# A fused attention and gated feed-forward kernel: the warm-up of TensorE as one chain of five groups, and a new written order

## The chip, the cores and the metric

The kernel runs on one core of one Trainium2 chip. A core has five engines, each with a queue of its own that it works through in order: PE (TensorE, matrix products, with PEld for its weight loads), DVE (VectorE), ACT (ScalarE), POOL (GpSimd) and SP (SyncE, which here only issues transfers). SP, ACT and POOL can issue DMA transfers; all of them run on the same 16 DMA engines. The metric is the device time of one execution, in microseconds, as the median of several runs.

## The reference

Two stages. The first is an attention in Nyström form for 8 batches of 8 heads, 576 tokens of 64 values: queries and keys are averaged over groups of 18 tokens into 32 landmarks, three softmax matrices are built, and the small one, 32 x 32, is inverted by six steps of an iteration.

```python
q_lm = q.reshape(B, H, m, S // m, D).mean(axis=3)
k_lm = k.reshape(B, H, m, S // m, D).mean(axis=3)
A = sm(q, k_lm); Bm = sm(q_lm, k_lm); C = sm(q_lm, k)
Z = Bm.T / (norm_1(Bm) * norm_inf(Bm) + 1e-06)
for _ in range(6):
    Z = 2 * Z - Z @ Bm @ Z
attn = A @ Z @ C @ v
```

The second takes the 4608 tokens of 512 values through a multiplicative feed-forward layer:

```python
a = x @ w1; b = x @ w2
out = (a * b @ w3) @ w_out
```

## The kernel before

**Parts.** `w3 @ w_out` is formed once on the chip: the products `mm{j}{c}` (j and c from 0 to 7) accumulate `w34`. Both factors are split into a high and a low half-precision part. For that, pieces of `w_out` (loads `wf0` to `wf3`, half issued by SP, names ending in `s`, half by ACT, ending in `a`, two DMAs each) go through `woh` and `wos` on ACT and `wol` on POOL; pieces of `w3` (loads `w3n0` to `w3n7`, on SP, half of the first on ACT) go through a transposition `tr` on DVE, `wh` and `ws` on ACT and `wl` on POOL. `mm{j}{c}` is three matmuls: high by high, high by low, low by high. So `mm00` needs `wh00`, `woh0` for its first matmul, `wol0` for its second and `wl00` for its third; `mm01`, `mm02`, `mm03` need `wol1`, `wol2`, `wol3`.

The attention works on 16 quads (four heads of one batch; n from 0 to 15). Loads `lq{n}0` and `lq{n}1` bring k and q, issued by POOL; `lv{n}` brings v, issued by SP. DVE transposes them (`T`), PE sums 18 rows for the landmarks of the first six quads (`mp{n}`, 18 matmuls; POOL does it for the others, `ma` and `mb`), ACT scales the sums (`mk`), DVE transposes those (`lt`), PE forms the scores (`S`, `A`), and the softmax passes through DVE (`sm`, `ar`, `am`, `au`), POOL (`as`, `an`) and ACT (`se`, `ae`). Then come the 32 x 32 iteration (`N`, `x`, `Z` on PE, `y` on DVE), the products with v (`C`), with w1 and w2 (`W`, `U`), the dense products (`d` on PE, `e` on ACT, `f` on DVE) and the output (`g` on PE, `h` on ACT, stores `st` on SP).

**Order.** Every step is a task with a name, an engine and a function. The string ORDER lists all of them; `Plan.run` reads names and buffer slots from it, and the kernel issues the tasks in just that order, so that each engine's queue is the part of ORDER that belongs to it. The dependencies, durations and due times that `add` is given are for the planner with which the order was made; `Plan.run` uses of a task its function and the names of its buffers (`acq`). What a task waits for on the chip follows from the tiles that it reads and writes. The number after a colon is a slot: a PSUM bank for PE's tasks, a buffer otherwise.

```python
def run(self):
    order = []
    for word in ORDER.split():
        name, _, slots = word.partition(":")
        t = self.by[name]
```

**Warm-up.** `zz` zeroes a tile on DVE, and `wu0` to `wu3` multiply it by itself, six matmuls of 128 x 512 each, into banks that nothing reads. `ca`, `cb`, `cc` build the identity and other constants on DVE, POOL and DVE. `gw0` to `gw3` are copies of one column on POOL; each reads the last bytes of a `wf` load, and so holds back what POOL issues behind it.

**The first tasks of each queue**, as ORDER before has them:

```
PE   wu2 wu3 wu0 wu1 mm00 mm01 mm02 mm03 mp0 mm04 mm05 mm06 A0 mm10 S0 mp1 mm07
ACT  w3n0a.0 w3n0a wf0a.0 wf0a wf1a.0 wf1a wf2a.0 wf2a wh00 ws00 woh1 wos1 wf3a.0 wf3a woh2 woh0
POOL cb gw0 wl00 wol1 gw1 lq00 lq01 lq10 lq11 wol0 wl01 wol2 wol3 wol4 gw2 wol5 gw3 wol6 wl10 lq20
DVE  tr00 ca zz tr01 cc tr10 T00 T01 tr11 lt0
SP   w3n0.0 w3n0 wf0s.0 wf0s wf1s.0 wf1s wf2s.0 wf2s w3n1 (4) wf3s.0 wf3s w3n2.0 w3n2.1 lv0.0
```

Of the kernel before, what the change touches and what calls it, by code (L numbers as in the profile page):

```python
# [44 lines left out]
woh7 A0:6.7 lq20:2 mm10:0 wos7 lq21 ar0:0 w3n3 ws11 S0:1.2 wol7 w3n4.0:1 T11 mp1:3 lv0.2 am0:0 lq30:3 w3n4.1
mm07 sm0:1 mk1:1 w3n4.2 as0 mm11 w3n4 tr20:0.0 sw0 mm12 wl11 lt1 ae0 tr21:1 mm13 wh20 au0 w3n5.0:2 lq31 wh21
A1:5.6 ws20 w3n5.1 S1:7.3 sb0 ar1:1 an0:0 ws21 mm14 se00:0 am1:2 mm15 wl20 se01 mm16 sm1:3 w3n5.2 mm17 as1 T20:0
sw1 ct0:0 mm20:5 wl21 ae1 mm21 tr30:2.1 wo0 aT0:0 mp2:6 w3n5 lq40:0 bo0:0 sb1 T21 lq41 mm22 au1 mk2:0 lq50:1
mm23 lq51 mm24 se10:1 lt2 lq60:2 T30:1 wh30 A2:1.2 lq61 tr31:3 ws30 mm25 lw00 T31 bo1 w3n6.0:0 mm26 wo1 wl30
w3n6.1 ar2:0 se11 mm27 lv0 wh31 an1:1 N0:4.4 w3n6.2 am2:5 wo2 S2:6.7 lv1.0:1 ws31 bt0 mm30:0 tr40:0.0 w3n6 as2  # L50
mm31 lv1.1 ct1:1 wh40 mp3:3 sm2:6 lw11 ae2 tr41:1 lw01 mp4:1 mk3:1 lv1.2 au2 wl31 mm32 ws40 T40:0 mm33 lq70:3
wh41 aT1:1 lq71 sw2 mk4:0 mm34 w3n7.0:1 sb2 lt3 an2:0 no0:0 mm35 se20:0 A3:2.5 ws41 wl40 lt4 T41 mm36 bo2:1 mm37
ar3:1 lv1 lw10 mm40:3 wl41 wo3 am3:7 S3:1.6 w3n7.1 tr50:2.1 x0_0:4 as3 A4:2.5 sm3:8 wh50 mm41 T50:1 ws50 lq80:0
sw3 mm42 ae3 tr51:3 ma6:0 w3n7.2 mp5:0 sb3 T51 ar4:0 mm43 w3n7 mk5:1 mm44 au3 wl50 se21 S4:2.5 am4:9 wh51 mm45
an3:1 lv2.0:2 se30:1 mm46 ct2:2 ws51 mm47 sm4:0 as4 bo3 lv2.1 se31 mm50:0 lt5 wo4 y0_0:1 tr60:0.0 sw4 lq81
A5:7.1 lv2.2 ct3:3 lq90:1 wh60 mm51 wl51 ae4 tr61:1 mm52 ws60 ar5:1 mm53 lq91 lv2 aT3:2 mm54 wl60 am5:2 mm55 au4
lv3.0:3 mm56 as5 S5:6.4 sb4 T60:0 x0_1:3 mb6 ae5 C0:1.7 sm5:4 wh61 lv3.1 au5 ws61 bo4 se40:0 T61 mm57 T70:1 wl61
sw5 mk6:0 mm60:2 lv3.2 co0:0.5 mm61 an4:1 lt6 mm62 y0_1:2 sb5 T71 se50:1 mm63 ma7:0 lv3 wo5 aT4:3 A6:1.7
tr70:2.1 bo5 se51 x0_2:3 N1:6.7 wh70 lv4.0:0 y0_2:0 ct5:0 S6:0.4 ws70 x0_3:3 an5:1 bt1 mm64 se41 ar6:0 lv4.1
mm65 no1:1 wl70 mm66 lv4.2 mm67 mb7 tr71:3 y0_3:2 x1_0:5 wh71 T80:0 lv4 x0_4:1 mm70:7 ws71 y1_0:0 y0_4:1 mm71  # L60
aT5:4 lv5.0:1 sm6:1 x1_1:6 wl71 mk7:1 Z0:3 am6:3 sw6 mm72 lv5.1 sb6 y1_1:2 as6 se60:1 mm73 lt7 zo0:0 se61 ct4:1
S7:5.1 lv5.2 ma8:0 ae6 W0:6 sm7:5 mm74 wp0:0 wo6 T81 lv5 A7:0.3 mm75 ar7:1 mb8 sw7 C1:4.2 T90:1 sb7 au6 se70:0
am7:9 bo6:0 se71 mm76 lv6.0:2 wq0 as7 T91 lv6.1 mk8:0 mm77 lv6.2 co1:1.2 U000:0.3.0.1 lv6 lq100:2 wo7 U011:5.1
lv7.0:3 aT2:5 ae7 U010:6.2 ma9:0 lt8 lv7.1 ct6:2 C2:4.7 uo0001 lv7.2 uo0110 ct7:3 lv7 uo0101 au7 uo0000 an6:1
uo0100 U001:3.5 uo0111 co2:0.7 lv8.0:0 S8:2.0 lv8.1 uo0011 lq101 d000:6.1 lv8.2 sm8:6 bo7 mb9 uo0010 lv8
d002:4.7 e000:0 lv9.0:1 sw8 f000:0 A8:5.3 lv9.1 e002:1 sb8 d021:6.1 f002:1 se80:1 lv9.2 ar8:0 d011:4.7 se81 lv9
e021:2 T100:0 d020:2.0 an7:0 am8:8 x1_2:3 e020:0 lq110:3 e011:1 d022:5.6 f021 mk9:1 lq111 f011 d001:2.4 y1_2:1
as8 f020 d010:1.7 e022:2 e001:1 f022 d032:3.5 e010:0 ma10:0 lt9 ae8 f001 d031:0.2 f010 e032:2 x1_3:6 e031:1 T101
d012:1.4 f032 lq120:0 d030:3.7 y1_3:0 e012:0 f031 lq121 A9:0.5 e030:2 aT7:0 lq130:1 x1_4:6 f012 mb10 S9:1.2
ar9:1 g30:3 sm9:2 g31 am9:0 g20:4 y1_4:2 T110:1 as9 sw9 mk10:0 f030 Z1:0 aT6:1 g21 sb9 ct8:0 ae9 ma11:0 g10:5  # L70
lt10 h3:0 zo1:1 h2:1 S10:6.7 au8 se90:0 W1:3 W2:0 au9 mb11 C3:4.1 wp2:1 wp1:0 bo8 se91 wq1 bo9 sm10:4 wq2 T111
U100:2.3.2.3 lv10.0:2 N2:0.3 lv10.1 ct9:1 uo1001 an8:0 lv10.2 uo1000 sw10 co3:1.7 g11 lv10 mk11:1 an9:1 lv11.0:3
bt2 A10:3.2 sb10 no2:1 lv11.1 se100:1 g00:1 lv11.2 ma12:0 h1:2 lv11 ar10:0 U110:4.6 se101 st1.0 U200:0.5.0.1
uo1101 lt11 st1 am10:9 x2_0:7 uo2001 st2.0 S11:2.3 uo2000 y2_0:0 as10 U210:6.5 T120:0 uo1100 A11:7.0 uo2100
sm11:1 g01 lq131 uo2101 T121 ae10 mb12 sw11 d200:4.6 sb11 ar11:1 se110:0 x2_1:5 h0:3 U201:2.0 se111 y2_1:2
U111:7.1 ct10:2 uo2010 x2_2:5 am11:5 e200:1 uo1110 d100:3.2 f200:2 as11 uo1111 U211:4.7 y2_2:1 e100:0 au10
U101:6.1 mk12:0 lq140:2 C4:5.3 f100 ae11 ma13:0 uo1011 au11 uo2111 uo1010 d101:2.1 lv12.0:0 lt12 uo2011 co4:0.8
st3.0 S12:7.6 lq141 e101:2 x2_3:0 lv12.1 uo2110 f101:3 lq150:3 d112:3.5 lv12.2 sm12:7 mb13 st3 d132:2.4 e112:1
y2_3:0 st0.0 sw12 f112 d121:1.3 e132:0 lv12 sb12 T130:1 se120:1 d111:0.5 lv13.0:1 e121:2 f132 st0 d202:2.7 se121
st2 e111:1 d110:1.4 e202:0 lv13.1 f111 d120:6.0 f121 e110:1 d130:2.5 f110 d231:3.1 T131 e130:2 e120:1 f202:0  # L80
x2_4:4 mk13:1 f120 d222:2.6 f130 d131:7.0 y2_4:2 e222:0 ma14:0 e231:1 d232:5.4 f222 e131:2 f231 d211:2.3 f131
d210:6.7 e211:0 e232:1 d122:1.0 f211 bo10:1 e210:2 d102:2.5 bo11 f210 e122:0 g60:3 aT8:2 e102:2 an10:0 f102
d201:6.1 ct11:3 g61 e201:2 mb14 f201 Z2:7 A12:2.5 zo2:0 d230:6.1 f122 T140:0 g50:7 e230:2 h6:2 ar12:0 lq151
d221:0.6 mk14:0 lt13 g40:3 am12:0 e221:0 lt14 g80:2 as12 T141 g70:5 f232 f221 g81 aT9:5 f230 d220:0.4 h8:0 g41
st8.0 ma15:0 st6.0 W4:6 h4:3 W3:1 st8 ae12 g71 lv13.2 wp3:1 e220:1 lv13 wq3 d212:2.3 ct12:0 st4.0 an11:1 g110:0
e212:0 f220 wp4:0 f212 h7:1 A14:1.2 mb15 g51 ar14:1 U300:4.3.2.3 aT10:3 h5:0 wq4 S14:5.1 uo3001 am14:3 st5.0
S13:2.7 uo3000 g90:6 st4 sm13:2 as14 st6 T150:0 g111 st7.0 sm14:6 ae14 sw13 st7 g91 sb13 T151 st5 se130:0 g120:3
au12 g121 au14 bo12 an12:0 h11:3 g100:4 h12:2 sw14 se131 g101 mk15:1 ct13:1 A13:2.0 sb14 aT11:4 h9:1 C6:3.7
ar13:0 se140:1 h10:0 am13:8 bo14:0 se141 lt15 as13 U301:6.0 co6:0.9 lv14.0:0 U400:2.5.0.1 lv14.1 uo3010 an14:1
U410:4.1 st11.0 uo4000 S15:3.7 ae13 lv14.2 C5:6.2 st12.0 uo4100 au13 uo4001 lv14 uo4101 lv15.0:1 sm15:5 uo3011  # L90
st10.0 bo13 U411:4.5 co5:1.0 st9.0 N3:1.2 uo4111 lv15.1 uo4110 sw15 st12 bt3 A15:0.2 sb15 no3:1 se150:0 lv15.2
d412:6.5 st10 se151 d402:4.3 ar15:1 e412:2 st11 x3_0:1 e402:1 st9 U401:7.6 f402:3 d400:0.2 uo4011 f412 uo4010
am15:7 d410:4.3 e400:0 d411:5.6 as15 e410:1 f400:1 d430:7.0 y3_0:0 e411:2 f410 d420:4.2 ae15 d422:1.5 e430:0
e420:1 f430 d431:3.7 f420 d432:4.0 f411 au15 g180:2 e432:0 e422:1 d421:6.4 e431:2 f422 g181 f431 e421:1 f432
f421 x3_1:1 h18:2 U311:3.5 st18.0 U310:7.6 g210:0 uo3100 uo3101 g211 uo3111 d310:4.2 h21:0 d401:7.6 st21.0
e310:2 uo3110 d300:5.0 f310 bo15 y3_1:2 e401:0 d321:4.3 f401 d301:2.1 e321:1 N4:7.9 e301:2 x3_2:6 e300:0 f301:2
d322:4.2 bt4 y3_2:1 d330:5.1 no4:0 e322:2 g190:6 f322 d320:4.7 f300 aT14:2 g191 e320:2 an15:1 f320 d311:2.0 f321
g200:4 e311:0 f311 d302:7.3 ct15:0 g201 e302:2 ct14:1 h19:3 d331:2.0 h20:1 d312:7.6 e330:1 st20.0 e331:0 f330
d332:4.5 st19.0 e312:1 g130:2 st18 f312 st21 aT12:5 g140:1 e332:1 f302 st19 an13:0 f331 g141 st20 x3_3:7 x4_0:6
# [940 lines left out]
```

## Time and profile before

| | us |
|---|---|
| median of 3 runs | 273.0 |
| lowest and highest | 271.47, 273.58 |
| profiled execution | 273.78 |
| its span | 272.0 |
| PE, DVE, ACT, POOL busy | 256.0, 179.7, 173.6, 137.6 |

The rows of the page and of the views that matter stand in the prediction. Times in them are from the start of the span. A timeline row is: start, length, engine and line, operation, written and read tile, how many instructions were merged, and in brackets how long the engine had been idle and what ended that. An engine's name with a q (ACTq, SPq) is its sequencer, which issues DMAs. Almost all matmuls have one line, L244, so tiles tell them apart: `bank<-aT` is the warm-up, `bank<-wo,w3t` the `mm` products, `bank<-nat,ident` the `mp` sums. `w3n`, `u` and `ab` are also the tiles into which weights are first loaded; `nat` takes k and q.

### The profile page before, as it was taken

To read this page: it belongs to the slowest core of one execution; us is meant where nothing else is said; L and a number is where in the kernel's file an instruction comes from. 1 tells how busy PE (TensorE), PEld (TensorE's weight loads), DVE (VectorE), ACT (ScalarE), POOL (GpSimd) and SP (SyncE) were. 2 spreads that over 40 slices of the span, in tenths; PEclk is the share of its full clock that TensorE was granted. 3 is DMA by queue.
4 is the path that set the end of the run, shared out by engine and by line. 5 is a ranking of instruction groups with operands and counts; after the bars stand their busy time and mean duration, and the time that the engine had idled before them with its cause. 6 is when DMAs were issued, how large, how long until landed. Compare 5 with 4: busy or idle time off the path is not lost.

```text
span 272.0 us, 9712 instructions
## 1 busy us (share of the span) xinstructions
PE 256.0 (94%) x4020; PEld 171.0 (63%) x4020; DVE 179.7 (66%) x446; ACT 173.6 (64%) x438; POOL 137.6 (51%) x151
## 2 busy tenths in 40 slices
...
POOL 0598899999999999999466713100110000000000
PEclk9997999999999999999999999999999999999998
...
GB/s 209 255 214 247 190 153 201 247 247 253 264 161 115 252 183 116 166 116 118 245 5 60 143 81 171 140 23 22 9 113 94 68 22 78 83 36 2 96 175 116
DMA packets 22668, 37.33 MB, mean 137 GB/s; under 512 B 3552, under 2 KB 7904, under 8 KB 22624
## 3 DMA queue, kind: packets, MB, share of 16 engines
...
q0 software_dynamic: 5696, 11.54, 24.2%
...
## 4 chain that ended last, share of the span: by engine, by line
PE 88%; DMA 5%; ACT 2%; issue 1%; POOL 1%; DVE 0%; DVEq 0%; POOLq 0%
PE bank L244 88%; DMA nat<-in_q_dram 3%; DMA u<-in_moe_w_out_dram 1%; DMA w3n<-in_moe_w_dram 1%; ACT L339 0%; POOL w3t L353 0%; ACT u L804 0%; ACT lm L481 0%; ACT asb L879 0%; DVE tiny L580 0%; POOL nat L420 0%; ACT osb L347 0%; ACT w3t L339 0%; ACT ea L574 0%; ACT osb L920 0%
## 5 line engine op out<-in xcount | busy, mean ns | idle before, releaser
L885 DVE TENSOR_TENSOR ab<-asb,bank 128x384 f16<-128x384 f16 x96 | 49.6, 544 | 42.9 <-ACT asb L879 37.2
L244 PE MATMUL bank<-aT,u 128*128 128x192 f16 x768 | 70.0, 246 | 0.0
L244 PE MATMUL bank<-w,ab 128*128 128x512 f16 (+1 forms) x296 | 69.6, 374 | 0.0
L244 PEld LDWEIGHTS <-u 128*128 128x128 f16 x768 | 63.8, 98 | 7.4 <-issue 0.7
L879 ACT CAST asb<-bank 128x384 f16<-128x384 f32 x96 | 43.8, 489 | 24.6 <-PE bank L244 19.4
L244 PE MATMUL bank<-wo,w3t 128*128 128x512 f16 x192 | 46.9, 384 | 2.9 <-POOL wo L326 2.9
L244 PEld LDWEIGHTS <-ab 128*128 128x128 f16 x296 | 27.5, 98 | 25.6 <-issue 2.1
L804 ACT CAST u<-bank 128x512 f16<-128x512 f32 x64 | 33.7, 607 | 6.1 <-PE bank L244 6.1
L899 ACT ACTIVATE osb<-bank 128x512 f32<-128x512 f32 x35 | 20.5, 600 | 22.5 <-PE bank L244 22.5
L594 POOL TENSOR_TENSOR ah<-ea,tiny 128x576 f16<-128x576 f32 x16 | 18.6, 1165 | 28.0 <-DVE aT L603 24.7
L244 PEld LDWEIGHTS <-w3t 128*128 128x128 f16 x192 | 18.2, 101 | 22.1 <-issue 5.4
L460 POOL TENSOR_TENSOR ls<-ls 128x128 f32<-128x128 f32 (+2 forms) x40 | 29.2, 731 | 2.6
L445 DVE STREAM_TRANSPOSE T<-nat 128x576 f32<-128x576 f32 x32 | 24.1, 755 | 6.5 <-DMA nat<-in_k_dram 5.4
L566 POOL TENSOR_TENSOR ea<-ea,tiny 128x608 f32<-128x608 f32 x16 | 19.4, 1214 | 15.6 <-DVE tiny L560 15.6
L453 POOL TENSOR_TENSOR ls<-nat 128x1152 f32<-128x1152 f16 x10 | 23.8, 2376 | 5.7 <-ACT lm L481 3.9
L353 POOL TENSOR_TENSOR w3t<-osb,w3t 128x512 f16<-128x512 f32 x16 | 18.7, 1166 | 2.7 <-ACT osb L347 2.6
L530 ACT ACTIVATE ec<-bank,tiny 128x288 f32<-128x288 f32 x32 | 16.1, 503 | 4.9 <-DVE tiny L522 4.8
L244 PE MATMUL bank<-T 32*32 32x288 f16 (+1 forms) x320 | 18.3, 291 | 0.2 <-DVE tiny L682 0.2
L244 PE MATMUL bank<-vb,ecT 64*64 64x128 f32 x576 | 17.7, 272 | 0.0
L244 PE MATMUL bank<-w,wT 64*32 64x512 f16 x512 | 17.3, 379 | 0.0
L244 PEld LDWEIGHTS bank<-vb,ecT 64*64 64x64 f32 x576 | 15.8, 133 | 1.9 <-issue 1.1
L332 DVE STREAM_TRANSPOSE osb<-w3n 128x512 f32<-128x512 f32 x16 | 11.0, 685 | 8.6 <-DMA w3n<-in_moe_w_dram 8.6
...
## 6 DMA issues: line engine op xcount, KB each, us to landing
...
```

Source lines behind the costliest of these rows:

```text
L244: nc.tensor.matmul(out_, lhsT, rhs, start=start, stop=stop, **({} if pos is None else {"tile_position": pos}))
L353: nc.gpsimd.tensor_tensor(out=t[:, 1, 4 * h:4 * h + 4].rearrange("p e g i -> p (e g i)"), in0=w3f[at(f"w3f{j}{h}")], in1=t[:, 0, 4 * h:4 * ...
L445: nc.vector.transpose(out=Ts[at(f"T{n}")][:, GRP * t:GRP * t + GRP] .rearrange("p r l e -> p (r l e)").bitcast(FP32), in_=nats[at(f"nat{n} ...
L453: nc.gpsimd.tensor_tensor(out=l, in0=nat[:, :, 0:9, :], in1=nat[:, :, 9:18, :], op=ALU.add)
L460: nc.gpsimd.tensor_tensor(out=l[:, :, x:x + m, :], in0=l[:, :, x:x + m, :], in1=l[:, :, y:y + m, :], op=ALU.add)
L530: nc.scalar.activation(out=ecs[at(f"ec{n}")][:, hp, :], in_=two(f"pS{n}")[hp][:, 0:288], func=AXF.Exp, scale=SCALE, bias=t[:, 2 + hp:3 + h ...
L566: nc.gpsimd.tensor_tensor(out=ea, in0=ea, in1=tinies[at(f"ta{n}")][:, 0:19].unsqueeze(2).to_broadcast([128, 19, M]), op=ALU.subtract)
L594: nc.gpsimd.tensor_tensor(out=ahs[at(f"ah{n}")].rearrange("p g m r -> p g r m"), in0=eas[at(f"ea{n}")][:, 0:GRP, :].rearrange("p (g r) m - ...
L804: nc.scalar.copy(out=uu[at(f"u{b}{qd}")][:, wi, 512 * half:512 * half + 512], in_=bank(at(f"pU{b}{wi}{half}{qd}")))
L879: nc.scalar.copy(out=asb[at(f"as{b}{j}{ch}")], in_=d1_ps(b, j, ch)[0])
L885: nc.vector.tensor_mul(abts[at(f"ab{i // 2}")][:, 2 * j:2 * j + 2, CH * (i % 2):CH * (i % 2) + CH], asb[at(f"as{b}{j}{ch}")], d1_ps(b, j, ...
L899: nc.scalar.activation(out=osb[at(f"os{i}")], in_=bank(at(f"pE{i}")), func=AXF.Copy, scale=2.0 ** -12)
```

## The change

It adds a fifth warm-up group, lists each group as depending on the one before it, makes `mm00`, the other `mm{j}0` and the `mp` steps depend on the fifth, makes `ca` depend on `zz`, and replaces the whole of ORDER.

```diff
-    for x in range(4):
-        add(f"wu{x}", "PE", 2.6 if x < 2 else 1.3, lambda x=x: warm(x), deps=["zz"], acq=[("P", f"pwu{x}", 1)], rel=[f"pwu{x}"],
-            at=("z", -5.0 + 2.0 * x), mode="full", kind="wu", n=2 * WARM)
+    for x in range(5):
+        add(f"wu{x}", "PE", 2.6 if x < 2 else 1.3, lambda x=x: warm(x), deps=[f"wu{x - 1}" if x else "zz"],
+            acq=[("P", f"pwu{x}", 1)], rel=[f"pwu{x}"], at=("z", -5.0 + 2.0 * x), mode="full", kind="wu", n=2 * WARM)
...
-    add("ca", "DVE", 0.2, const_a, at=("z", -10.0))
+    add("ca", "DVE", 0.2, const_a, deps=["zz"], at=("z", -10.0))
...
-                if c:
-                    deps.append(f"mm{j}{c - 1}")
+                deps.append(f"mm{j}{c - 1}" if c else "wu4")
...
-            add(f"mp{n}", "PE", 0.98, mean_mm(n), deps=loads + ["cc"], acq=[("P", f"pM{n}", 1)],
+            add(f"mp{n}", "PE", 0.98, mean_mm(n), deps=loads + ["cc", "wu4"], acq=[("P", f"pM{n}", 1)],
```

The start of ORDER, old and new:

```diff
-w3n0a.0 w3n0.0:0 w3n0a w3n0 wf0a.0 wf0s.0 wf0a wf0s wf1a.0 wf1s.0 wf1a wf1s wf2a.0 wf2s.0 wf2a wf2s w3n1.0:1
-tr00:0.0 w3n1.1 ca wh00 zz cb w3n1.2 tr01:1 wu2:0 ws00 cc woh1 gw0 w3n1 wl00 wu3:1 wos1 wf3s.0 wf3a.0 wol1 wf3a
-wu0:2 wf3s woh2 gw1 woh0 lq00:0 w3n2.0:2 wh01 lq01 woh3 w3n2.1 lq10:1 wos0 lq11 lv0.0:0 wu1:3 wos2 wol0 ws01
-wos3 w3n2.2 wl01 woh5 w3n2 woh4 mm00:4 wol2 tr10:2.1 lv0.1 wos4 mm01 wos5 wol3 mm02 w3n3.0:0 T00:0 wol4 mm03
...
+w3n0a.0 w3n0.0:0 w3n0a w3n0 wf0a.0 wf0s.0 wf0a wf0s wf1a.0 wf1s.0 wf1a wf1s wf2a.0 w3n1.0:1 wf2a wf2s.0 wf3a.0
+wf2s wf3a tr00:0.0 w3n1.1 zz wh00 w3n1.2 ca wu0:0 tr01:1 cb ws00 cc woh1 gw0 w3n1 wl00 wos1 wf3s.0 wh01 wol1
+wu1:1 woh0 wf3s woh3 gw1 lq00:0 woh2 lq01 ws01 w3n2.0:2 wos2 lq10:1 wu2:2 wos0 w3n2.1 wol2 woh5 w3n2.2 lq11
+wu3:3 w3n2 woh4 gw2 wol0 w3n3.0:0 wos4 wu4:4 wos3 tr10:2.1 w3n3.1 wl01 wh10 mm00:5 wol3 wos5 lv0.0:0 mm01 T00:0
...
```

By queues the new order begins like this:

```
PE   wu0 wu1 wu2 wu3 wu4 mm00 mm01 mm02 mm03 mp0 mm04 mm05 mm06 S0 A0 mp1 mm07
ACT  w3n0a.0 w3n0a wf0a.0 wf0a wf1a.0 wf1a wf2a.0 wf2a wf3a.0 wf3a wh00 ws00 woh1 wos1 wh01 woh0
POOL cb gw0 wl00 wol1 gw1 lq00 lq01 lq10 wol2 lq11 gw2 wol0 wl01 wol3 wol5 wol4 wol6 wl10 gw3 lq20
DVE  tr00 zz ca tr01 cc tr10 T00 tr11 T01 lt0
SP   w3n0.0 w3n0 wf0s.0 wf0s wf1s.0 wf1s w3n1.0 wf2s.0 wf2s w3n1 (3) wf3s.0 wf3s w3n2 (4) w3n3.0 w3n3.1 lv0.0
```

Later on the same tasks stand in each queue in another order, with other PSUM banks.

More of the change, by code (lines that the diff above doesn't have):

```diff
@@ L45 @@
[L45 to L99, printed above, removed]
@@ new lines @@
+wu3:3 w3n2 woh4 gw2 wol0 w3n3.0:0 wos4 wu4:4 wos3 tr10:2.1 w3n3.1 wl01 wh10 mm00:5 wol3 wos5 lv0.0:0 mm01 T00:0
+ws10 mm02 tr11:3 wol5 woh6 w3n3.2 mm03 wol4 wos6 mp0:6 T01 wol6 mm04 mk0:0 w3n3 mm05 wl10 mm06 woh7 lt0 T10:1
+wos7 gw3 S0:7.0 lq20:2 A0:1.2 wh11 sm0:0 lv0.1 wol7 mp1:3 ar0:0 lv0.2 lq21 w3n4.0:1 mm07 mk1:1 am0:1 w3n4.1 sw0
+mm10:4 w3n4.2 as0 ws11 lt1 mm11 w3n4 tr20:0.0 mm12 wl11 T11 ae0 mm13 wo0 au0 lq30:3 wh20 A1:6.1 lq31 mm14 ws20
+ar1:1 mm15 wl20 tr21:1 S1:2.3 T20:0 wh21 w3n5.0:2 mm16 an0:0 w3n5.1 sm1:2 ws21 mm17 w3n5.2 bo0:0 sb0 wl21 mp2:5
@@ new lines @@
+w3n5 aT0:0 am1:3 sw1 tr30:2.1 mm20:1 mk2:0 as1 mm21 wh30 lq40:0 mm22 lt2 T21 ae1 lq41 mm23 sb1 tr31:3 se00:0
+lq50:1 A2:6.5 ws30 au1 lq51 w3n6.0:0 mm24 wh31 w3n6.1 lq60:2 mm25 wo1 T30:1 lv0 an1:1 ws31 mm26 w3n6.2 ar2:0
+se01 w3n6 S2:7.4 wl30 lv1.0:1 T31 mm27 lv1.1 am2:4 mp3:0 lq61 sm2:5 wl31 mm30:5 mk3:1 tr40:0.0 mm31 lw10 tr41:1
+mm32 wh40 as2 lt3 w3n7.0:1 T40:0 mm33 ws40 w3n7.1 se10:1 mm34 T41 lq70:3 wh41 mm35 lq71 ct0:0 ae2 lw00 mm36
+lv1.2 bo1 au2 ws41 lw01 A3:6.0 se11 sw2 wl40 mm37 lv1 ar3:1 wo2 mp4:2 tr50:2.1 wl41 am3:6 mp5:3 mk4:0 an2:0
@@ new lines @@
+T60:1 se50:0 an4:0 lv3 y0_2:0 se51 tr70:2.1 x0_3:3 bo4 wl61 au5 mm60:4 wh70 lv4.0:0 mm61 ws70 lq90:1 T61 bo5
+mm62 ma7:0 y0_3:1 lv4.1 lt6 mm63 T70:0 mm64 co0:0.4 lv4.2 x0_4:5 S6:0.3 ct5:0 wl70 mm65 sb4 T71 lv4 se40:1
+N1:2.6 mb7 tr71:3 mm66 bt1 lv5.0:1 wh71 sm6:0 mm70:6 se41 no1:2 mm71 ws71 lv5.1 mm72 y0_4:0 A6:7.1 ct4:1 an5:1
+mk7:1 lv5.2 mm67 ar6:0 sw6 wl71 x1_0:2 T80:1 lv5 mm73 sb6 lt7 lq91 se60:0 y1_0:1 Z0:5 T81 ma8:0 S7:1.7 se61
+x1_1:2 am6:2 A7:0.3 sm7:9 mm74 y1_1:2 mm75 as6 zo0:0 T90:0 W0:2 sw7 aT4:4 wp0:0 mb8 mm76 ae6 wq0 sb7 ar7:1 mm77
@@ new lines @@
+C1:5.2 au6 wo7 se70:1 wo6 am7:4 se71 T91 as7 bo6:0 mk8:0 U000:0.3.0.1 lv6.0:2 co1:1.6 U011:6.1 lv6.1 lq100:2
+U010:4.7 ct6:2 ae7 lv6.2 lq101 C2:2.5 lv6 lt8 uo0110 au7 an6:0 lv7.0:3 uo0111 lv7.1 uo0000 aT5:5 lv7.2 lq110:3
+uo0101 ct7:3 lv7 uo0100 lq111 A8:6.1 lv8.0:0 co2:0.3 uo0001 ma9:0 U001:0.7 lv8.1 ar8:0 lv8.2 S8:4.3 uo0011
+d000:2.5 uo0010 sm8:5 d002:7.1 lv8 e000:0 am8:8 lq120:0 sw8 d021:6.0 e002:1 sb8 f000:0 mb9 se80:0 d011:2.7
+lv9.0:1 T100:1 e021:2 se81 d010:5.4 f002:1 bo7 f021 e011:0 x1_2:6 lv9.1 e010:1 ct8:0 d032:3.1 y1_2:0 d012:0.2
@@ new lines @@
+d430:0.3 uo3100 e411:2 f402:3 d410:7.5 as15 f411 d432:1.4 e410:0 d422:6.2 f410 e432:1 e430:2 d431:7.5 e422:0
+f430 U311:1.0 f422 e431:2 x3_0:6 uo3111 f431 d412:3.2 ae15 f432 ct15:1 d420:7.0 uo3110 e412:0 d421:5.4 e420:2
+f412 d401:1.3 y3_0:1 f420 g210:7 e401:1 aT12:2 au15 g211 d301:2.6 an15:0 h21:2 e421:0 x3_1:0 st21.0 f421
+d310:1.7 st10.0 f401 d302:5.4 st10 e310:2 e301:0 g200:3 st5 f301:2 st21 g180:1 y3_1:2 g181 d322:2.6 g201 e322:1
+h18:3 f322 d300:0.2 h20:1 f310 d321:1.6 e302:0 f302 d320:3.7 e321:1 g190:5 e320:2 e300:0 g191 f300 f320 d330:4.1
```

67 lines of the change are left out of this document (49 added, 18 removed).

## The prediction

> **What bounds the kernel now.** I read the page first, then the waits of TensorE, then the chain that ended last, then stretches of the span cut at the points that the chain names, and last the timelines of ACT, POOL, DVE and PE over the first 29 us.
>
> ```profile
> span 272.0 us, 9712 instructions
> ...
> PE 256.0 (94%) x4020; PEld 171.0 (63%) x4020; DVE 179.7 (66%) x446; ACT 173.6 (64%) x438; POOL 137.6 (51%) x151
> ...
> POOL 0598899999999999999466713100110000000000
> ...
> PEclk9997999999999999999999999999999999999998
> ```
>
> The span is 272.0 us and the profiled execution took 273.78, so 1.78 lie outside the span. PE is busy for 256.0. In 40 slices of 6.8 us the granted clock has one dip, in the fourth (20.4 to 27.2 us), and POOL is busy for nine tenths or more from 34 to 129 us.
>
> ```profile
> PE bank L244 <- DVE aT L262: 6.3, 1, 6.3
> PE bank L244 <- POOL wo L326: 2.9, 3, 1.8
> PE bank L244 <- DMA nat<-in_q_dram: 1.2, 1, 1.2
> PE bank L244 <- issue: 0.7, 1, 0.7
> ```
>
> Columns: total us, times, longest. PE waits for the zeroed tile of the warm-up (6.3), then for POOL's weight remainders (the `wol` steps, 2.9), then for a load of q (1.2); in all the rest it idles 0.9.
>
> ```profile
> 7.15 1.27 ACT L339
> ...
> 8.43 0.64 ACT w3t L339
> ...
> 9.80 1.16 POOL w3t L353
> ...
> 12.14 0.19 POOL gates L376
> 12.32 0.65 POOL nat L420
> 12.97 7.83 DMA nat<-in_q_dram
> ...
> 20.94 98.60 PE bank L244 x1585
> ```
>
> This is the chain, start and length. It does not pass through the warm-up. It runs from ACT's first work (7.15, a table load, then `wh00` and `ws00`) to POOL (`wl00`, then `wol1`, `gw1` and the loads `lq00`, `lq01`), through 7.83 us of transfer, to `mp0` on PE at 20.94. From there PE is the chain nearly to the end.
>
> ```profile
> 13.61:20.94 7.33, 3.24 (x14) 1.00 1.08 215
> 20.94:24.34 3.40, 3.40 (x22) 0.50 1.10 269
> 24.34:124.30 99.96, 99.96 (x1827) 1.00 0.87 189
> 125.40:267.23 141.83, 141.13 (x2128) 1.00 0.36 85
> ```
>
> Columns: length, PE busy, clock, share of the DMA engines, GB/s. Three things are left to win or lose: the idle part of 13.61 to 20.94 (4.1), the half clock of 20.94 to 24.34 (3.40 at half speed, so 1.7), and some 0.9 of idling later. The DMA engines are full (1.08, 1.10) while this is decided.
>
> **The code first.** `P.run` reads ORDER alone. The added dependencies (`wu` in a chain, `wu4` ahead of `mm00` and of the `mp` steps, `zz` ahead of `ca`) enter no instruction; PE runs its queue in order anyway. What changes on the chip is six more matmuls and five queues in a new order.
>
> **Fifth group and earlier zero.**
>
> ```profile
> 5.72 0.17 DVE L255 MEMSET ident<- 128x128 f32 x1
> 5.90 0.30 DVE L262 MEMSET aT<- 128x288 uint32 x1
> ```
>
> ```profile
> 6.25:10.68 4.43, 4.43 (x11) 1.65 (x12) 2.86 (x25) 3.41 (x5) 1.07 (x3) 1.00 1.06 260
> 10.68:13.90 3.22, 3.22 (x16) 1.36 (x14) 0.71 (x1) 2.90 (x7) 3.15 (x6) 1.00 1.02 243
> ```
>
> `zz` now runs ahead of `ca`, so the warm-up starts 0.18 earlier, at 6.07; `cb` and `cc` behind `ca` start up to 0.3 later, and `mp0`, the first to need them, is the last thing that PE waits for anyway. The matmuls go at 4.43/11 = 0.40 us each until 10.68 and 3.22/16 = 0.20 after it. Thirty of them: 11 to 10.5, then 19 x 0.20 to 14.4. The first group that can wait is `mm00`, whose second matmul needs `wol0`:
>
> ```profile
> 15.82 1.46 PE L244 MATMUL bank<-wo,w3t 128*128 128x512 f16 x6 [1.82 <-POOL wo L326]
> ...
> 20.94 2.08 PE L244 MATMUL bank<-nat,ident 128*128 128x128 f16 x18 [1.21 <-DMA nat<-in_q_dram]
> ...
> 27.17 1.18 PE L244 MATMUL bank<-nat,ident 128*128 128x128 f16 x18
> ```
>
> Before, PE stood until 15.82 for it. The sixth group of 1.2 us therefore costs nothing; if `wol0` were ready at 13.6 it would cost 1.2 - 0.2 = 1.0.
>
> **ACT: `wf3a` moves ahead of the first activation.** This is the step that I weigh most. Before, ACT issued eight DMAs, then `wh00 ws00 woh1 wos1`, then the two halves of `wf3a`. Now it issues ten DMAs and then `wh00`.
>
> ```profile
> 1.68 0.93 ACTq L299 DMA_DIRECT2D u<-in_moe_w_out_dram  x2
> ```
>
> ```profile
> 3.80 1.37 ACTq L299 DMA_DIRECT2D u<-in_moe_w_out_dram  x2
> 5.78 1.32 ACTq L299 DMA_DIRECT2D ab<-in_moe_w_out_dram  x2
> 7.13 1.28 ACT L339 ACT_TABLE_LOAD   x1 [7.13 <-DMA u<-in_moe_w_out_dram]
> ...
> 10.35 0.80 ACTq L299 DMA_DIRECT2D ab<-in_moe_w_out_dram  x2
> ```
>
> ```profile
> L307 ACTq DMA_DIRECT2D w3n<-in_moe_w_dram x2: 423/437/451, 0.7 to 1.2; - x2
> ...
> DMA to landing us min/median/max: 3.0/3.3/3.6
> ```
>
> ACT issues four DMAs until 2.61 and then stands. The fifth goes at 3.80 and the sixth at 4.85; the first two had been issued at 0.74 and 1.20 and landed 3.0 and 3.6 later, at 3.78 and 4.83. So each issue waits for the landing of ACT's fourth DMA before it, and all that is queued behind it on ACT waits too. By that, the ninth and tenth wait for the fifth and sixth:
>
> ```profile
> 4.85 0.32 ACTq L299 DMA_DIRECT2D u<-in_moe_w_out_dram  x1
> ```
>
> ```profile
> L299 ACTq DMA_DIRECT2D u<-in_moe_w_out_dram x1: 318/318/318, 4.9 to 4.9; - x1
> ...
> DMA to landing us min/median/max: 3.7/3.7/3.7
> ```
>
> The sixth landed at 4.85 + 3.7 = 8.55; the tenth issue ends at 8.87, and the table load starts there instead of at 7.13: +1.74. If the tenth waited only for the fifth (3.80 + 3.7 = 7.5), it would end at 7.8: +0.7. No wait at all: two issues, +0.64. I take 1.74. Queued behind are `wh00`, `ws00`, `woh1`, `wos1`; the chain above shows who waits: POOL's `wl00` (9.80 to 11.54), then `wol1`, `gw1`, `lq00`, and `lq01` from 12.97 to 14.71.
>
> **POOL: `wol2` and `gw2` move ahead of `wol0`, `wol2` also ahead of `lq11`.**
>
> ```profile
> 14.57 1.20 POOL L326 TENSOR_TENSOR wo<-u,wo 128x512 f16<-128x512 f32 x1
> 15.69 1.18 POOL L353 TENSOR_TENSOR w3t<-osb,w3t 128x512 f16<-128x512 f32 x1
> 16.81 2.28 POOL L326 TENSOR_TENSOR wo<-u,wo 128x512 f16<-128x512 f32 x2
> ...
> 20.14 0.18 POOL L376 COPY gates<-ab 128x1 f32<-128x1 f32 x1
> ```
>
> `wol0` started at 14.57: now 14.57 + 1.74 + 1.14 (`wol2`) + 0.18 = 17.63, done 18.83 instead of 15.77. `wol3` ended at 19.09; now `wol0`, `wl01` and `wol3` at 1.12 apart end at 21.03. So `mm00` stands until 18.9 and `mm03` until 21.05. `lq11` is issued 1.74 + 1.14 later, but it queues behind three other loads, so its landing moves by about 1.74. None of this passes the later of the two ends: `mp0`.
>
> **The load.** `lq01`: 14.71 + 7.83 = 22.54, `mp0` at 22.68 instead of 20.94. From below: hardware loads that have run ahead leave it a larger share, and `mm03` is then the last, 21.5. SP's swap (`w3n1.0` ahead of `wf2s`, `w3n2` and `w3n3` ahead of `lv0`) changes which 128 KB come first, not the bytes; `lv0` is first read by `C0`, some seventy tasks later on PE.
>
> **The clock.** Before, 20.94 to 24.34 ran at half: full-speed work began, as it were, at 20.94 + 1.7 = 22.64. Now PE has nothing from about 14.4 to 18.9, where before the longest pause was 1.8 and the clock still fell. (a) If it falls at 20.9 and returns at 24.34 again: 22.68 + 0.83 = 23.51, +0.9. (b) If it falls before `mm00`: 11 matmuls x 0.40 from 18.9 end at 23.3, and half of the rest to 24.34 is 0.5: 23.8, +1.2. (c) If, with PE not full in 20.9 to 24.3, it returns one step of 3.4 later, at 27.75: 22.68 + 2.5 = 25.2, +2.6. (d) If it never falls: +0.0.
> The Trainium skill (TensorE: Matmul & The Clock Gate, Part 1: The HAM clock gate) says that the clock is halved after at least one idle window of about 3.4 us, in windows that run freely. The trace agrees with the step (3.40) but not with the condition: it fell with no pause of that length. By the rule taken strictly a pause of 4.5 need not hold a whole window, and (d) is what it would then give.
>
> **The rest of PE's work.** I counted both orders: the same tasks, and 101 changes of tile size on PE in each. The places where PE needs another engine's result within 0.2 us of its being due, by the mean times of the page, are 10 before and 8 after. I take it as unchanged: +0.0, from -0.9 (all later idling goes) to +4 (the 1.74 by which POOL is late, met twice or so at such hand-offs).
>
> **Sum.** Between (a) and (b): +1.1 on 273.78, 274.9. The profiled execution is 0.8 above the median of the three runs (273.0, from 271.47 to 273.58), by which the sum would be 274.1; I give 274.5.
>
> **Rivals.** *The clock holds* (d): the longer warm-up does its work, +0.0: 273.0 to 273.8. For it: 0.40 to 0.20 is what it buys. Against: the pause after it is longer than before. *Faster:* ACT's wait does not come, because the landings are earlier, and the clock holds: -1.7, and -0.9 of later idling: 270.4 to 271.2. Against: four issues in the trace wait in this way. *Clock late* (c): +2.6: 275.6 to 276.4. [...] *A late stall:* POOL is full to 129 us, and starts 1.74 late; where its results are due within less than the amount by which PE is late, PE waits a second time: +1.1 and +3: 277 to 278.
>
> **Chances.** Forecast 0.44, clock holds 0.14, faster 0.12, clock late 0.17, late stall 0.13. The range leaves out the faster half of the fast rival and the end of the last: 271.8 to 277.6. One per cent (2.7 us) is about what can be told from no change. Faster by more: half of the fast rival and a little, 0.08. Slower by more (above 275.7): the last two, 0.28, and the upper end of the forecast, 0.02: 0.30. Within: 0.62.
>
> **What would show it.** The table load at 8.8, `wl00` at 11.5, `lq01` issued at 14.7, `mp0` at 22.7 (by the tile `nat` on PE), and a half clock around 21 to 24. The warm-up's end at 14.4 and PE's wait for `wo` ending at 18.9. It is wrong if the table load comes at 7.1 to 7.8, or if PE's waits after 30 us come to more than 2.

## The result and the profile after

The changed kernel took 274.06 us (median of 20 runs, 273.5 to 276.22), the kernel before 272.46 beside it (20 runs, 270.85 to 277.82): a ratio of 1.0075, 95% interval 1.0052 to 1.0098. Ratios, here and below, are of the means over the undisturbed executions, which leave out the 277.82 of before; that of the two medians is 1.0059. It is slower, by less than one per cent. The profiled executions tell less of this than the medians: 274.0 after and 273.78 before, since the one before was 1.3 above its own median and the one after at its median.

The page after, its span and the rows that answer to those shown of before:

```profile
span 272.2 us, 9735 instructions
...
PE 256.5 (94%) x4026; PEld 171.1 (63%) x4026; DVE 180.7 (66%) x446; ACT 173.4 (64%) x438; POOL 137.6 (51%) x151
...
PEclk9997999999999999999999999999999999999999
```

Six more matmuls, and one dip of the clock in the same slice as before. The waits of PE (total, times, longest):

```profile
PE bank L244 <- DVE aT L262: 6.1, 1, 6.1
PE bank L244 <- POOL wo L326: 4.8, 1, 4.8
```

The wait for `wo` has grown from 2.9 to 4.8 in one piece; the wait for q's load (1.2) and the late 0.7 with no releaser are gone. ACT's timeline after shows why POOL is late:

```profile
6.24 3.09 ACTq L299 DMA_DIRECT2D ab<-in_moe_w_out_dram  x4
9.37 1.28 ACT L339 ACT_TABLE_LOAD   x1 [9.37 <-DMA ab<-in_moe_w_out_dram]
10.66 0.63 ACT L339 ACTIVATE w3t<-osb 128x512 f16<-128x512 f32 x1
```

Before, the table load stood at 7.13. The table load and `wh00` behind it are 2.24 and 2.23 later. POOL's timeline after:

```profile
12.04 1.16 POOL L353 TENSOR_TENSOR w3t<-osb,w3t 128x512 f16<-128x512 f32 x1 [4.44 <-ACT osb L347]
...
15.21 0.54 POOL L419 DMA_DIRECT2D nat<-in_q_dram  x1
...
18.21 1.17 POOL L326 TENSOR_TENSOR wo<-u,wo 128x512 f16<-128x512 f32 x1
```

`wl00` (9.80 before), the issue of `lq01` (12.97) and `wol0` (14.57): all later by 2.24, the last by 1.4 more. And PE's timeline:

```profile
14.28 0.38 PE L244 MATMUL bank<-wo,w3t 128*128 128x512 f16 x1
19.43 4.22 PE L244 MATMUL bank<-wo,w3t 128*128 128x512 f16 x11 [4.76 <-POOL wo L326]
23.48 1.17 PE L244 MATMUL bank<-nat,ident 128*128 128x128 f16 x18
```

`mm00` begins, stands for `wol0` until 19.43, then `mm00` to `mm03` run, and `mp0` comes at 23.48 instead of 20.94, 2.54 later. What the clock did is in the stretches of the span (length, PE busy, clock, DMA share, GB/s):

```profile
14.45:19.40 4.95, 0.21 (x1) 1.00 1.13 237
...
19.80:23.22 3.42, 3.42 (x10) 0.50 1.12 238
...
125.40:267.43 142.03, 142.03 (x2184) 1.00 0.37 86
```

The eleven products had 0.4 us of full clock and then ran at half until 23.22. From 125.40 on PE does not pause, where before it lost 0.70; PE ends at 267.43 instead of 267.23. So in the profiled pair the 2.54 lost at `mp0` stand against a half clock that is over by then (before, it cost 1.7 after `mp0`), which leaves 0.84, and against the late pause of 0.70; PE's end is only 0.20 later.

### The profile page after: what moved, and what is told of

It reads as the page before. It is cut to its first block, busy times and chain, and to the rows that moved or that the text cites. A ratio compares the mean times of both kernels' runs of the same rounds, so it can differ in the third digit from the quotient of the medians.

```text
span 272.2 us, 9735 instructions
## 1 busy us (share of the span) xinstructions
PE 256.5 (94%) x4026; PEld 171.1 (63%) x4026; DVE 180.7 (66%) x446; ACT 173.4 (64%) x438; POOL 137.6 (51%) x151
## 3 DMA queue, kind: packets, MB, share of 16 engines
q0 software_dynamic: 5696, 11.54, 24.3%
## 4 chain that ended last, share of the span: by engine, by line
PE 90%; DMA 4%; POOL 2%; ACT 1%; issue 1%; ACTq 0%; POOLq 0%
PE bank L244 90%; DMA ab<-in_moe_w_out_dram 2%; DMA u<-in_moe_w_out_dram 2%; DMA w3n<-in_moe_w_dram 1%; POOL nat L419 1%; POOL wo L326 1%; ACT lm L480 0%; ACT ab L321 0%; POOL gates L376 0%; ACT wo L315 0%; ACTq L307 0%; ACT osb L919 0%; ACT lm L478 0%; POOLq L376 0%
## 5 line engine op out<-in xcount | busy, mean ns | idle before, releaser
L244 PE MATMUL bank<-w,ab 128*128 128x512 f16 (+1 forms) x296 | 68.9, 374 | 0.0
L898 ACT ACTIVATE osb<-bank 128x512 f32<-128x512 f32 x35 | 20.9, 604 | 15.9 <-PE bank L244 15.5
L452 POOL TENSOR_TENSOR ls<-nat 128x1152 f32<-128x1152 f16 x10 | 23.8, 2377 | 2.3 <-issue 1.6
L353 POOL TENSOR_TENSOR w3t<-osb,w3t 128x512 f16<-128x512 f32 x16 | 18.5, 1161 | 4.9 <-ACT osb L347 4.8
L244 PEld LDWEIGHTS bank<-xz 32*32 32x32 f32 x768 | 13.0, 104 | 6.9 <-issue 1.6
```

The costliest lines, as they stand in the source:

```text
L244: nc.tensor.matmul(out_, lhsT, rhs, start=start, stop=stop, **({} if pos is None else {"tile_position": pos}))
L353: nc.gpsimd.tensor_tensor(out=t[:, 1, 4 * h:4 * h + 4].rearrange("p e g i -> p (e g i)"), in0=w3f[at(f"w3f{j}{h}")], in1=t[:, 0, 4 * h:4 * ...
L452: nc.gpsimd.tensor_tensor(out=l, in0=nat[:, :, 0:9, :], in1=nat[:, :, 9:18, :], op=ALU.add)
L898: nc.scalar.activation(out=osb[at(f"os{i}")], in_=bank(at(f"pE{i}")), func=AXF.Copy, scale=2.0 ** -12)
```

## The experiments

Theory: the loss is the delay of ACT's first activation by `wf3a`, through POOL and `mm00` to `mp0`; the fifth group and the rest of the new order do next to nothing. Rivals: POOL's order (`gw2` and `wol2` ahead of `wol0`), the pause with its half clock, or the new order further on. Ratios are to runs of the kernel before on the same chip. The edits of ORDER are shown by queue; where nothing is said, the rest of each queue is unchanged.

**wf3a back behind the first activations, in the changed kernel.**

```diff
-ACT  w3n0a.0 w3n0a wf0a.0 wf0a wf1a.0 wf1a wf2a.0 wf2a wf3a.0 wf3a wh00 ws00 woh1 wos1
+ACT  w3n0a.0 w3n0a wf0a.0 wf0a wf1a.0 wf1a wf2a.0 wf2a wh00 ws00 woh1 wos1 wf3a.0 wf3a
```

> The changed kernel with one move undone: ACT's two loads of the last weight piece (wf3a) go back behind its first four activations. Theory W (ACT's queue stands for the landing of its fifth and sixth load, and POOL, the loads of k and q and the weight remainders follow it): the first activation at 8.4 instead of 10.66 us, POOL's first remainder at 9.8 instead of 12.04, lq01 issued near 13.0 instead of 15.2, mp0 near 21 and, after the half clock, the unbroken work of PE 1 to 1.5 us earlier; ratio to before 1.002 to 1.004 instead of 1.0075. Rival B (the DMA engines are full, so the bytes decide when k and q land): ACT starts early but mp0 moves by less than 0.3; ratio 1.006 to 1.009.

Measured: 272.27 against 271.93, ratio 1.0017, interval 0.9992 to 1.0041. ACT's timeline, PE's timeline and its stretches in this run:

```profile
7.72 1.28 ACT L339 ACT_TABLE_LOAD   x1 [7.72 <-DMA u<-in_moe_w_out_dram]
```

```profile
18.13 2.82 PE L244 MATMUL bank<-wo,w3t 128*128 128x512 f16 x11 [3.56 <-POOL wo L326]
20.79 1.17 PE L244 MATMUL bank<-nat,ident 128*128 128x128 f16 x18
```

```profile
16.38:19.80 3.42, 1.67 (x8) 1.00 1.08 199
19.80:23.21 3.41, 2.87 (x27) 1.00 1.09 256
```

The table load is 1.65 earlier than in the changed kernel, the products that wait for `wol0` 1.30, and `mp0` comes at 20.79, 2.69 earlier: the first theory's 21, and not the rival's 23.2 or more. In this execution the clock does not fall in the start, and PE ends at 265.28, 2.15 earlier. Over the run's 12 executions the mean granted clock goes from 0.983 to 0.999, so that the clock held in all of them is not shown. One edit of two DMA issues takes the loss down to what can't be told from nothing. All the rest of the change, five groups and the other queues, is in this run.

**The same move alone, on the kernel before.**

```diff
-ACT  w3n0a.0 w3n0a wf0a.0 wf0a wf1a.0 wf1a wf2a.0 wf2a wh00 ws00 woh1 wos1 wf3a.0 wf3a
+ACT  w3n0a.0 w3n0a wf0a.0 wf0a wf1a.0 wf1a wf2a.0 wf2a wf3a.0 wf3a wh00 ws00 woh1 wos1
```

> The kernel before with only this done: ACT's two loads wf3a ahead of its first activation. Theory W: first activation near 10.4 instead of 8.43, lq01 issued 2 us later, mp0 at 22 to 22.7 instead of 20.94, of which 0.8 to 1.2 us reach the end: ratio 1.003 to 1.005. Rival B: mp0 as before, ratio 0.999 to 1.001.

Measured: 273.53 against 271.93, ratio 1.0055, interval 1.0035 to 1.0075. The chain of this run:

```profile
8.93 1.28 ACT L339
...
14.77 7.10 DMA nat<-in_q_dram
...
22.00 4.08 PE bank L244 x33
```

Against the timelines of before, the table load is 1.80 later (7.13 there), `lq01`'s issue 1.80, `mp0` 1.06. The loss of time itself stands in the run's executions and not in its trace: the profiled one (273.29) was faster than the profiled one of before (273.78, which was 1.3 above its median), and PE ended earlier in it, at 266.75. So the move costs on either order: 0.55% alone, and 0.17% is left for all else. Within their intervals the two add up to the 0.75% of the whole change.

**Four groups instead of five, in the changed kernel.**

```diff
-PE   wu0 wu1 wu2 wu3 wu4 mm00
+PE   wu0 wu1 wu2 wu3 mm00
```

> The changed kernel with the warm-up back at four groups, the rest of the new order kept. Theory W: PE stands 4.8 us for wol0 behind the warm-up, so the fifth group hides in that wait: ratio to before 1.006 to 1.009, mm00's second matmul at the same 19.4. Rival F (the fifth group itself costs its 1.2 us): ratio 1.003. Rival C (the fifth group shortens the cold stretch): the clock falls a step earlier, slower by 0.3 to 1 us, ratio 1.009 to 1.011.

Measured: 274.2 against 271.93, ratio 1.0083, interval 1.0055 to 1.0111. PE's wait in this run:

```profile
PE bank L244 <- POOL wo L326: 4.8, 1, 4.8
```

It is the same 4.8, and the clock falls too (at 18.45). The fifth group neither costs nor gives anything that can be told within this interval: it ends inside the wait for `wol0`.

**A fifth group that fills the pause.**

```diff
-        for _ in range(WARM):
+        for _ in range(WARM if x < 4 else 28):
```

> The changed kernel with 28 matmuls instead of 6 in the fifth warm-up group, so that the warm-up ends near 19.2 us, just before wol0 comes. Theory C (the half clock from 19.8 to 23.2, which follows from PE's pause, makes mm00 to mm03 last until 23.5): no half clock before the real products, mm03 then ends with wol3 near 22.0 and mp0 starts with lq01 near 22.2 instead of 23.48; 1 to 1.3 us less, ratio to before 1.003 to 1.004. Rival P (POOL's work decides from there on, since mm07 waited for wol7 until 28.9): mp0 earlier but mm07 at the same 28.5 and nothing gained, ratio 1.007 to 1.008.

Measured: 275.22 against 271.93, ratio 1.0122, interval 1.0088 to 1.0156. Neither expectation held. The warm-up ran to 20.1, the clock held, and `mp0` came at 22.74, 0.74 earlier than in the changed kernel; but the time did not fall. A second run with a shorter fill looked for the reason, on another chip:

```diff
-        for _ in range(WARM):
+        for _ in range(WARM if x < 4 else 24):
```

> The changed kernel with 24 matmuls in the fifth group (28 were 1.0122 times before, with the clock held and 0.74 won at mp0). Theory (what cost time there was a wait tied to the place in PE's list of instructions and a longer tail, not the held clock): warm-up ends near 18.2, clock does not fall, mp0 near 22.7, the wait at the weight load near 205 us is gone or moves, ratio 1.003 to 1.007. Rival (holding the clock early is paid back later whatever the place): ratio 1.009 or above again.

Measured: 274.68 against 272.44, ratio 1.0077, interval 1.0053 to 1.0101, which lies between the two expectations. The warm-up ended at 18.5, the clock held, and `mp0` came at 21.86, 1.62 earlier than in the changed kernel. Waits of this run:

```profile
PE bank L244 <- ACT ec L529: 0.4, 1, 0.4
...
ACT osb L919 <- DMA out_dram<-osb: 0.9, 1, 0.9
```

Followed task by task against the changed kernel, the lead is 1.28 at `mp2`, 0.77 from `x0_3` on (68 us; the wait for `ec`), 0.30 from `W5` on (206 us; the wait with no releaser), and 0.30 at PE's end. Two of the last evictions on ACT stand for a store, but the last one still ends 0.26 earlier than the changed kernel's (267.59 against 267.85). What loses the rest is SP: one of its last store issues lasts 1.64 (264.32 to 265.96) where none of the changed kernel lasts more than 0.59, those behind it follow without a gap, the last comes at 269.23 instead of 268.91, and the span ends 0.3 later. The run with 28 has such an issue too (1.66, from 264.53), and its last eviction waits as well, in its chain:

```profile
262.93 4.06 DMA out_dram<-osb
...
267.15 0.66 ACT osb L919 x2
```

A store that landed 4.06 after its issue (the page of the changed kernel gives 2.4 as the median) held the tile that the last eviction needs. So a held clock, worth more than a microsecond at `mp0`, was given back at three places further on. Why the landing and the issue took longer is not settled. These two kernels, and no other, load a 32nd block of instructions (the queue `q8 instruction` of their pages has 32 transfers, the others 31), from 264.0 to 265.6 and from 264.2 to 265.8, at the time of the long issue; that it causes it is not shown. And why the run with 28 was slower than the one with 24 isn't settled either.

**Six more warm-up matmuls alone, on the kernel before.**

```diff
-        for _ in range(WARM):
+        for _ in range(2 * WARM if x == 1 else WARM):
```

> The kernel before, its order unchanged, with six more warm-up matmuls in the last of its four groups: the fifth group's work alone. Theory W: the warm-up ends near 14.9 instead of 13.8, still ahead of wol0 (15.8), so ratio 0.999 to 1.001 in the start. Rival F (the group costs its time): ratio 1.004. A second question is PE's wait of 0.78 us for nothing that the profile shows, between the two halves of sw15 near 169 us: if it belongs to the work there it stays at that place, if it belongs to the place in PE's list of instructions it moves or goes, worth up to 0.8 us.

Measured: 272.18 against 272.55, ratio 0.9997, interval 0.9964 to 1.0029. Here `wu1` is the last group in PE's queue. The clock held in the profiled execution, and `mp0` came at 21.23, but no difference in time can be told. One wait of PE grew:

```profile
PE bank L244 <- issue: 1.0, 1, 1.0
```

It stood at the same number in PE's list of weight loads (2639) as the 0.7 of before, and so six instructions earlier in the work; more of it below.

**wol0 ahead of wol2 and gw2, in the changed kernel.**

```diff
-POOL cb gw0 wl00 wol1 gw1 lq00 lq01 lq10 wol2 lq11 gw2 wol0 wl01 wol3
+POOL cb gw0 wl00 wol1 gw1 lq00 lq01 lq10 lq11 wol0 wl01 wol2 gw2 wol3
```

> The changed kernel with POOL's part put back for one stretch: lq11, wol0 and wl01 ahead of wol2 and gw2; ACT's part stays new. Theory W: the wait on ACT decides, and behind it the stretch from wol0 to mp0 is set by wol3 and the half clock. wol0 comes near 18.0 instead of 19.4, mm00 to mm02 are done before wol3, mp0 starts near 22.3 instead of 23.5, half of the gain is left after the clock returns at 23.2: 0.5 to 0.9 us less, ratio to before 1.004 to 1.006. Rival N (what ends the start is POOL's sum up to wol7, the same in either order): mm07 at the same 28.5, ratio 1.007 to 1.008.

Measured: 273.7 against 272.55, ratio 1.0033, interval 1.0005 to 1.0061. `wol0` starts at 16.78 instead of 18.21, `mm03` at 21.19 instead of 22.46, `mp0` at 22.82 instead of 23.48 and now waits for `lq01`, which landed at 22.68. The clock still fell, at 18.18. So POOL's order probably has a share once ACT is late, which the theory had put at next to nothing; the interval overlaps that of the whole change, so neither the share nor that it is smaller than ACT's is shown.

**wf2a later as well, on the kernel before.** If two issues ahead of the first activation cost, the two that were there already should cost too.

```diff
-ACT  w3n0a.0 w3n0a wf0a.0 wf0a wf1a.0 wf1a wf2a.0 wf2a wh00 ws00 woh1 wos1 wf3a.0 wf3a
+ACT  w3n0a.0 w3n0a wf0a.0 wf0a wf1a.0 wf1a wh00 ws00 wf2a.0 wf2a woh1 wos1 wf3a.0 wf3a
```

> The kernel before with two more loads of ACT (wf2a) moved behind its first two activations, the opposite of the change. Theory W: the table load at 5.2 instead of 7.1, first activation 6.5 instead of 8.43, POOL's first remainder near 8 instead of 9.8, lq01 issued near 11.3 instead of 13.0, mp0 at 19.2 to 20; ratio 0.993 to 0.997. Rival B (full DMA engines decide when k and q land): mp0 as before, ratio 0.999 to 1.001.

Measured: 271.43 against 272.55, ratio 0.9975, interval 0.9943 to 1.0007. ACT's timeline of this run:

```profile
6.57 0.63 ACT L339 ACTIVATE w3t<-osb 128x512 f16<-128x512 f32 x1
```

`wh00` is 1.86 earlier than before, `mp0` comes at 18.30 instead of 20.94, the clock held. PE ends at 264.68, 2.55 earlier, but the interval still takes in no gain at all.

**The table load taken out of the way.** A small activation on a tile of its own, zeroed first thing on DVE, stands behind ACT's fourth DMA issue, where ACT waits anyway; `wf2a` is late here as in the run above.

```diff
+    early = fixed.tile([128, 4], FP32, name="early")
...
+    add("dz", "DVE", 0.1, lambda: nc.vector.memset(early, 0.0))
+    add("da", "ACT", 0.2, lambda: nc.scalar.activation(out=early, in_=early, func=AXF.Copy, scale=1.0))
...
-ACT  w3n0a.0 w3n0a wf0a.0 wf0a wf1a.0 wf1a wf2a.0 wf2a wh00 ws00 woh1 wos1 wf3a.0 wf3a
+ACT  w3n0a.0 w3n0a wf0a.0 wf0a da wf1a.0 wf1a wh00 ws00 wf2a.0 wf2a woh1 wos1 wf3a.0 wf3a
```

> As the run before, and with a dummy activation on four columns behind ACT's fourth load, so that the 1.28 us of the table load fall into the time from 2.6 to 3.8 in which ACT stands for a landing. Theory W: first activation at 5.8, as soon as tr00 is done; POOL's first remainder near 7.1, lq01 another 0.5 to 1 us earlier; ratio 0.990 to 0.995. Rival B: no more than the run before.

Measured: 271.33 against 272.55, ratio 0.9944, interval 0.9913 to 0.9975: faster than both kernels. ACT's timeline of this run:

```profile
2.64 1.28 ACT L270 ACT_TABLE_LOAD   x1 [2.64 <-issue]
...
3.94 0.21 ACT L270 ACTIVATE early<-early 128x4 f32<-128x4 f32 x1
...
6.00 0.63 ACT L342 ACTIVATE w3t<-osb 128x512 f16<-128x512 f32 x1 [1.85 <-DVE osb L335]
...
8.49 0.63 ACT L318 ACTIVATE wo<-u 128x512 f16<-128x512 f32 x1 [1.20 <-DMA u<-in_moe_w_out_dram]
```

The 1.28 of the table load now lie where ACT waited for landings, and `wh00` waits for its data (DVE's transpose) and no longer for a DMA issue. Part of the gain is lost at once: `woh1`, behind `wf2a`, stands for 1.20. What the early table load is worth by itself this run does not show: the interval overlaps that of the run above (0.9943 to 1.0007), and against its trace `wh00` is 0.57 earlier, but `lq01`'s issue 0.28 later (11.87 against 11.59) and `mp0` 1.23 later (19.53 against 18.30); PE ends 0.36 earlier, and 0.50 of that is a shorter wait with no releaser.

**The same edits on the order planned anew,** with `wf3a` behind `wos1`.

```diff
-ACT  w3n0a.0 w3n0a wf0a.0 wf0a wf1a.0 wf1a wf2a.0 wf2a wf3a.0 wf3a wh00 ws00 woh1 wos1
+ACT  w3n0a.0 w3n0a wf0a.0 wf0a da wf1a.0 wf1a wh00 ws00 wf2a.0 wf2a woh1 wos1 wf3a.0 wf3a
```

> The order planned anew, with ACT's head mended: the table load behind ACT's fourth load by a dummy activation, wf2a and wf3a behind the first activations. Theory (the whole loss of the change is the delay of ACT's first work, and what was planned anew behind it is neutral): table load at about 2.7, wh00 at 6.0, lq01 issued at about 12 instead of 15.21, mp0 near 19.5, clock not falling; ratio 0.996 (0.993 to 0.999), about what the same edits gave on the order before (0.994). Rival (the new order is itself worse further on, so that an earlier start is lost again): ratio 0.999 or above, with mp0 near 19.5 all the same.

Measured: 271.84 against 272.44, ratio 0.9973, interval 0.9950 to 0.9996. With POOL's order of the run above on top of it:

```diff
-POOL cb gw0 wl00 wol1 gw1 lq00 lq01 lq10 wol2 lq11 gw2 wol0 wl01 wol3
+POOL cb gw0 wl00 wol1 gw1 lq00 lq01 lq10 lq11 wol0 wl01 wol2 gw2 wol3
```

> As the run before, with POOL's lq11, wol0, wl01 and wol2 ahead of gw2. Theory (wol0 gates mm00, and mm00 to mm03 gate mp0 when the load is early): wol0 done some 1.3 earlier, near 15.5; ratio 0.001 to 0.003 below the run before. Rival (POOL's order decides nothing once the load comes early, since mp0 waits for lq01): the same ratio within 0.001.

Measured: 271.79 against 272.44, ratio 0.9975, interval 0.9958 to 0.9992: no difference between the two that can be told, as the rival had it. In both the load of q decides again. The chain of the first:

```profile
25.69 7.48 DMA nat<-in_q_dram
...
33.31 232.04 PE bank L245 x3736
```

`mp0` came at 19.95, nearly as early as on the order before (19.53), but `mp2` waited for `lq21`, which POOL issues at 25.69, behind `wol7`. On the order before the load is issued at 23.41, ahead of `wol7`, and `mp2` does not wait. In the changed kernel as it was, PE was too late to meet this wait (`mp2` at 35.67). The intervals of the two versions overlap, so whether the order before is the better base is not shown.

## Why the prediction was right

The forecast of 274.5, a small loss, held, and so did the range. By its steps:

**The code first, fifth group.** Right. The added dependencies are nowhere to be seen; the fifth group ended at 14.45 (14.4 predicted) under the cover that was named, the wait for `wol0`, and the run with four groups shows no price of it that can be told.

**ACT.** The mechanism was right, its size too small: +2.24 measured, +1.74 predicted. The table load does start right behind the tenth issue, and that issue behind the landing of the sixth. The chain after shows the landings:

```profile
4.85 4.15 DMA u<-in_moe_w_out_dram
9.00 0.02 issue
9.02 4.21 DMA ab<-in_moe_w_out_dram
```

The sixth was issued at 4.85 as predicted, but took 4.15 to land, not 3.7: 9.00 instead of 8.55, and 9.00 + 0.32 + 0.05 is 9.37. The duration had been taken from one landing, and this one moves from run to run: in the run with the move alone the table load stood at 8.93, close to the 8.87 predicted. The two bounds below, +0.64 and +0.7, are ruled out by all runs with `wf3a` early.

The rule behind it, that each issue waits for ACT's fourth DMA before it, holds for the orders of before and after and not beyond them. In the trace each issue waits for a semaphore, eight of them are dealt in turn to the DMAs of ACT and SP together, and an issue goes 0.02 after the landing of the DMA that had its semaphore before. In the changed kernel the tenth issue of ACT shares a semaphore with its sixth. In the run with the early table load the fifth shares one with the first DMA of SP: that landed at 3.74 and the issue went at 3.76, while ACT's own first landed only at 3.97. So what an issue waits for is in the built program, and may be a transfer of another engine.

**POOL and the load.** The predicted times are off by the same 0.5: `wol0` done at 19.38 (18.83), `lq01` issued at 15.21 (14.71). The load then took 6.81 rather than 7.83 and landed at 22.02, earlier than the 22.54 forecast: the lower bound named in the prediction. So not `lq01` but `mm03` was last, and the load is no longer the later of the two ends. So the step "None of this passes the later of the two ends" failed: what makes `wol0` later still counts, which the prediction had taken as free. With `wol0` first `mp0` came 0.66 earlier; the ratio was 1.0033, though its interval overlaps that of the whole change.

**The clock.** Case (b) came: it fell before `mm00` was done, at 19.80, and returned at 23.22. The prediction had put the fall between 20.9 and 24.3 as before. It came 1.12 earlier, which fits a clock that had risen 1.12 earlier (9.56 instead of 10.68): from rise to fall it is 10.24 in both. Case (c) did not come in any run: in all five executions whose clock fell in the start it was back after one step, in the run with four groups though PE was busy for only 2.71 of the 3.41. For the start of full-speed work, as it were, (b) gave 23.8; measured is `mp0` at 23.48 with the clock back, 0.84 later than the 22.64 of before. But the half clock is not the price of the change: with the clock held by a longer fifth group, and `mp0` 1.62 earlier, the ratio was 1.0077. Nor is the dip the same in every execution: the mean granted clock ran from 0.985 to 1.000 over 20 executions of the kernel before (mean 0.994) and from 0.983 to 0.994 over 20 of the changed one (mean 0.991), where one half window takes 0.5 x 3.41/272 = 0.006. Nor does the time follow it: of the 75 executions of the kernel before on three chips that the ratios of the experiments count, those with a granted clock of 0.998 or more were only 0.14 to 0.21 us faster on average than those with 0.993 or less, chip by chip, where a half window taken at face value is 1.7. Part of this mean is a half clock behind PE's last product, at the end of the span, which costs nothing.

**The rest of PE's work.** Taken as +0.0, from -0.9; in the profiled pair it was the lower bound, the late 0.7 being absent in the new list; the last section shows what it goes with. The late stall that the rival named did not come: PE does not wait once after 29.34 us. Such waits show where PE is early: in the runs that filled the pause, and at `mp2` in the new order with an early table load.

**The sum.** For the profiled pair +1.1 was too much, by 0.9: 0.3 at the clock (23.8 against 23.48) and 0.6 at the later idling. For the medians, which differ by 1.6, it was 0.5 too little; the time came out near because the prediction set its sum between the profiled execution and the median of three runs. That is in part luck: by the median of 20 runs, 272.46, the same sum gives 273.6, below the 274.06 measured. The step that was mis-sized is ACT's term, 2.24 for 1.74, and the one that was wrong is POOL's, taken as free. Why the profiled execution of before was 1.3 above its median isn't settled; its clock, 0.990, was among the lower ones.
